# Four edits at the seams of a one-core kernel: start-up, down passes, first attention step, closing mix

## The chip, the core and the metric

The kernel runs on one core of one Trainium2 chip. The metric is the device time of one execution in microseconds (us); lower is better. The core has a matrix engine (PE, with PEld for its weight loads), two elementwise engines (DVE and ACT), a general engine (POOL), a queue engine (SP) and 16 DMA engines. SP, ACT and POOL can each issue DMAs, and each issues in the order of its own program.

## The reference, cut to what matters

```
x: [2048, 1024]   A_mem0: [8, 1024]   32 heads of 128   SEG = 32 -> 64 segments
g = sigmoid((x * gate_w).sum(-1))                    # one gate value per row
a: for each segment s, in order:
     h = concat(mem, x[32 s : 32 s + 32])            # 8 memory rows + 32 new rows
     q, k, v = h Wq, h Wk, h Wv                      # 1024 -> 32 heads x 128
     o = softmax(mask(q k^T / sqrt(128))) v ;  o = o Wo
     mem = o[0:8] ;  a rows of this segment = o[8:40]
b = (gelu(x Wg) * (x Wu)) Wd                         # 1024 -> 3584 -> 1024
out = g * a + (1 - g) * b
```

All tensors are bf16. Segment s + 1 needs the memory rows that segment s wrote, so attention is a chain of 64 steps.

## The kernel before, in words

A small planner class (`_Prog`) records every operation with the memory regions that it reads and writes. Each engine executes its operations in the order in which the code recorded them, and the class puts a semaphore wait on an operation wherever it depends on another engine or on a DMA. A DMA with a `lane` name also waits for the DMA before it in the same lane. So the order of the Python code is the order of each engine and of each queue, and a wait at the head of a queue holds up all that stands behind it there.

The work goes through four stages.

*Start-up.* Four tiles of x (128 rows each) are loaded on SP (`load_x`, L539). `do_x` turns each tile on PE (L550) into a PSUM bank. ACT (L557) and DVE (L558, L559) copy the turned tile out, ACT issues the stores of it to the scratch tensors `xq_scr` and `xr_scr`, POOL multiplies the tile with the gate weights (L566), and DVE sums the product (L568). `gate(0)` (L629 to L636) turns four sums into gate values and stores them from POOL, among others as single 4-byte values (`gt_scr`). Then the rows of the initial memory and the first segment are put together in `hT0` (`load_h`, L572, and the copy L663).

*Feed-forward stage.* Four blocks of 512 rows (`fb` 0 to 3). In each, 28 steps j run gate and up products on PE (L680) and a gelu on ACT and DVE (L688 to L696); the tile `xT` holds the block's input. Then two down passes (`ps` 0 and 1) of seven chunks each multiply the result with `w_down` (L732). A chunk is 16 matmuls of 128x512 and uses one 1 MB tile `wd`; there are three such tiles, and the load of the tile for chunk n + 3 (`load_wd`, L612, on SP) is issued when chunk n has been used. During the j steps of a block the four tiles of x of the next block are turned (`do_x`, at j = 3, 9, 15, 21), `gate` runs at j = 25, and in blocks 1 and 2 copies of attention weights between DRAM tensors are issued on SP (`spread`, L392). The load of `xT` for the next block (`load_xT`, L594, on SP, 1 MB) is issued after the last j. Results of the down passes are scaled and stored to `b_scr` (`mix`, L621 and L623).

*Attention steps.* The weights of k, q, v and o do not fit, so 50 slots of 4 KB per partition hold pieces of them; a slot whose piece has been used is loaded with the next one from SP (`spent`, L430). `walk` is the fixed order of the projections (L916, L932, L949) and `plan(s)` hangs the rest of step s at places in that order. The last 8 of each 32 new rows are projected four segments at a time in *fills* (L986): the result is copied out by ACT into a stage tile (`fill_evac`), and `fill_put` turns it on PE, copies it back on DVE and stores it from POOL to `qk_scr` (L1011, lane `fq`). In step 0 seven fills are done at once, with the stage tiles `kS`, `qS` and `oS`, which lie over `kT`, `qT` and `oT`. The step's scores (L839, L842) need part of `kT` that POOL copies (L1015) from `qkr`, which POOL loads back from `qk_scr` (L581). Each step stores its results to `a_scr` (L1129, on POOL).

*Closing stage.* `early` and the code after the walk load, for each of 16 row tiles T, 96 rows of `a_scr` (four DMAs of 96x256, L780) and 96 rows of `b_scr` (one DMA of 96x1024, L782), all on SP, into 6 pairs of buffers (`asb`, `bsb`). DVE mixes them with the gate (`blend`, L789) and ACT stores the rows (L792). The 8 remaining rows of each segment go through the output projection at the end (L1157, 256 matmuls) and are mixed at L1167.

In the profile the names of scratch tensors are shown without numbers, so `wall<-o_scr` is a weight piece of o read from its scratch copy, not the tensor `o_scr` of the steps.

Of the kernel before, what the change touches and what calls it, by code (L numbers as in the profile page):

```python
# [191 lines left out]
class _V:  # L192
# [11 lines left out]
    r = _T.r  # L204
# [6 lines left out]
def bass_gated_mix__memory_aug_recurrent_mem_tr__geglu_ffn__prompt_kernel(  # L211
# [34 lines left out]
    with ExitStack() as es:  # L246
# [16 lines left out]
        a_scr = nc.dram_tensor("a_scr", [NSEG, 4, SEG, 256], BF16)  # L263
# [254 lines left out]
        assert cur[0] == edge(50) and len(hosts) == 50  # L518
        tp = [al(f"tp{t}", [128, FB], FP32, at=qkr.off + 4 * FB * t) for t in range(2)]
# [21 lines left out]
        def do_x(T):  # L541
# [112 lines left out]
        load_w(1)  # L654
        for T in range(TB):
            do_x(T)
            load_x(T + NPX)
        gate(0)
# [3 lines left out]
        load_h(0, "pool")  # L662
        op("dve", lambda e: e.tensor_copy(hT0[:, :, NR:32], memT[:, :].rearrange("p (k c) -> p k c", k=KC)),  # L663
           rd=[memT.r()], wr=[hT0.r()])
        load_w(2)
        load_w(3)
        load_w(4)
        for n in range(3):
            load_wd()
        copies = [(m, u, i) for m in "ovkq" for u in (1, 0) for i in PAIRS[m]]  # L670
        todo = []
        for fb in range(NFB):
            HB, DN = ((0, 1, 2, 3), (4, 5, 6, 7)) if fb % 2 == 0 else ((4, 5, 6, 7), (0, 1, 2, 3))
            for j in range(NJ):
# [39 lines left out]
            if fb + 1 < NFB:  # L714
                load_xT(fb + 1)
            else:
                for n in (11, *range(20, 29)):
                    begin(n)
            for ps in range(NPS):
                bank = DN if ps == 0 else HB  # L720
                tbs = [x for x in (2 * ps, 2 * ps + 1) if x < TB]
                for c in range(NWD):
                    end = fb == NFB - 1
                    w = wdF if end else wd[((fb * NPS + ps) * NWD + c) % 3]
                    for jj in range(WD):
                        j = c * WD + jj
                        x = j if end else jj

                        def f(e, w=w, x=x, j=j, bank=bank, tbs=tbs):
                            for k, tb in enumerate(tbs):  # L730
                                for hf in range(2):
                                    ins = e.matmul(PB[bank[2 * k + hf]][:, :], lhsT=GT[:, j, tb * 128:(tb + 1) * 128],  # L732
                                                   rhs=w[:, x, hf * 512:(hf + 1) * 512], start=(j == 0), stop=(j == NJ - 1))
                            return ins
                        op("pe", f, rd=[GT.r(j * FB, (j + 1) * FB), w.r(x * D, (x + 1) * D)], wr=[BK(b) for b in bank[0:2 * len(tbs)]])
                        if j > 0 and todo:
                            mix(*todo.pop(0))
                    if not end:
                        load_wd()
                    elif ps == NPS - 1:  # L740
                        for n in (29 + 2 * c, 30 + 2 * c, 43 + c):
                            begin(n)
# [6 lines left out]
        oR = [al(f"oR{b}", [128, RB, 32], at=slots[home["q", 0, 0]].off + b * SB * 512) for b in range(NBK)]  # L749
# [7 lines left out]
        NA = 6  # L757
# [6 lines left out]
        assert cur[0] <= slots[home["v", 1, 5]].off  # L764
# [12 lines left out]
        def load_a(T):  # L777
            t, w = asb[T % NA], bsb[T % NA]
            for n in range(4):
                op("sp", lambda e, n=n: e.dma_start(t[0:NM, 256 * n:256 * n + 256], a_scr[4 * T:4 * T + 4, n, 0:NR, :]),  # L780
                   rd=[("D", "a", s) for s in range(4 * T, 4 * T + 4)], wr=[t.r(256 * n, 256 * n + 256)], lane=f"al{T % NA}{n}")
# [248 lines left out]
        def fill0(m, r, b, st, G=0, h=hR):  # L1030
            run(fill(m, r, b, h))
            fill_evac(m, r, G, b, st)
            fill_put(m, r, G, st)

        def plan(s):
# [44 lines left out]
            on(*(("q", 1, 1) if s else ("o", 0, 0)), lambda: evac(bank_of["k", 1], stage[ub if s else "k"], "act"))  # L1080
# [13 lines left out]
            else:  # L1094
# [4 lines left out]
                on("o", 0, 6, lambda: scores(ub, False))  # L1099
# [12 lines left out]
            if last:  # L1112
                for n, f in enumerate(early):
                    on(*((("v", 1, 4), ("o", 1, 0), ("o", 1, 1)) + (("o", 1, 2),) * 3)[n], f)
# [14 lines left out]
            on("k", 0, 4, lambda: op("pool", lambda e: e.dma_start(a_scr[s].rearrange("g r c -> (g r) c"), a_bf[:, :]), rd=[a_bf.r()],  # L1129
# [10 lines left out]
        op("pool", lambda e: e.dma_start(a_scr[NSEG - 1].rearrange("g r c -> (g r) c"), a_bf[:, :]), rd=[a_bf.r()],  # L1140
# [68 lines left out]
```

## Time and profile before

| what | value |
|---|---|
| time, median of 3 runs | 2300.27 us (2295.94 to 2300.56) |
| the profiled execution, its own time | 2304.75 us |
| its span, first to last instruction | 2302.9 us |
| PE busy | 2051.2 us, 89% of the span |
| DVE, ACT, POOL busy | 1042.1, 539.0, 434.2 us |
| start-up, until gate and up products run without a stall | 0 to 40 us |
| feed-forward stage | 40 to 649 us |
| attention step 0 | 650 to 709 us |
| steps 1 to 63 | 709 to 2178 us |
| closing stage | 2178 to 2303 us |

Busy time is the time in which an engine works on an instruction; it says nothing on what a stage waits for. Four views do: the chain that ended last, the sums of waits of an engine in a window, the timeline of a window, and the table of windows with the share of the 16 DMA engines in use.

### The profile page before, as it was taken

The page shows a single profiled execution, that of the slowest core. Times are in us where ns is not written, and L with a number is a line of the kernel's source. Part 1 is how long each engine was busy: PE and PEld are TensorE (multiplying, and loading weights), DVE is VectorE, ACT ScalarE, POOL GpSimd, SP SyncE. Part 2 cuts the span into 40 slices and gives each one's busy share as a digit, 9 for nine tenths or more (in the row PEclk, how much of TensorE's full clock was granted, in tenths as well). Part 3 has the DMA queues.
Part 4 walks back from the last instruction along what each step waited for, and adds up shares of the span by engine and source line. Part 5 has one row for each costly group of instructions (what it writes and reads, how often), then busy time and mean ns, then how long its engine had stood idle before and what let it go on. Part 6 is the DMA issues. An engine that isn't in the chain of part 4 may idle for free.

```text
span 2302.9 us, 69850 instructions
## 1 busy us (share of the span) xinstructions
PE 2051.2 (89%) x31365; PEld 975.8 (42%) x31365; DVE 1042.1 (45%) x2689; ACT 539.0 (23%) x1110; POOL 434.2 (19%) x839
## 2 busy tenths in 40 slices
PE   5999989999968999899999999999999989998880
PEld 2444434444424444444444444444444444444450
DVE  3624606516314445454545454555454544544412
ACT  2312303203112222222222222222222222222100
POOL 3000100000012222222222222222223222221100
PEclk8999999999989999999999999999999999998895
DMA  9255385293577899899999898999999989998932
GB/s 302 107 169 193 107 248 166 59 320 118 188 282 281 329 345 350 330 349 346 346 342 350 330 350 330 358 347 361 351 351 335 349 327 345 342 348 321 345 121 99
DMA packets 187871, 652.74 MB, mean 283 GB/s; under 512 B 22156, under 2 KB 78092, under 8 KB 146740
## 3 DMA queue, kind: packets, MB, share of 16 engines
q1 hardware_dynamic: 161060, 608.10, 72.6%
q0 software_dynamic: 14528, 26.32, 3.5%
q10 hardware_dynamic: 11984, 13.85, 1.7%
q8 instruction: 246, 4.03, 0.7%
q14 instruction: 53, 0.43, 0.1%
HBM read 613.64 MB, written 49.23 MB: 288 GB/s over the span
## 4 chain that ended last, share of the span: by engine, by line
PE 62%; DMA 21%; DVE 6%; SPq 5%; ACT 3%; issue 2%; POOL 1%; ACTq 0%; DVEq 0%; POOLq 0%
PE pb L916 24%; PE pb L680 13%; DMA wall<-o_scr 10%; PE pb L732 7%; PE pb L932 5%; PE pb L814 3%; SPq L780 3%; PE pb L949 3%; DMA o_scr<-oRc 3%; PE pb L986 2%; DMA wd<-in_B_w_down_dram 2%; DMA sl<-v_scr 1%; DVE oT L800 1%; PE pb L874 1%; DMA qk_scr<-1S 1%
## 5 line engine op out<-in xcount | busy, mean ns | idle before, releaser
L916 PE MATMUL pb<-sl,hT 128*32 128x512 bf16 x12288 | 763.9, 384 | 15.1 <-DVE hT L973 8.8
L916 PEld LDWEIGHTS pb<-sl,hT 128*32 128x32 bf16 x12288 | 308.5, 97 | 326.7 <-issue 27.7
L680 PE MATMUL pb<-xT,wg 128*128 128x512 bf16 x896 | 215.2, 384 | 21.8 <-DVE GT L696 15.6
L986 PE MATMUL pb<-sl,hR 128*32 128x512 bf16 x3072 | 212.9, 385 | 3.2 <-DVE osb L621 1.5
L680 PE MATMUL pb<-xT,wu 128*128 128x512 bf16 x896 | 212.3, 380 | 0.0
L949 PE MATMUL pb<-wall,oT 128*32 128x256 bf16 x4056 | 152.8, 280 | 28.0 <-DMA wall<-o_scr 23.7
L899 POOL COPY oRc<-oT 128x128 bf16<-128x128 bf16 x128 | 96.5, 754 | 402.4 <-DVE oT L800 402.4
L960 DVE COPY part<-pb 64x256 f32<-64x256 f32 x128 | 54.0, 422 | 257.4 <-PE pb L949 256.7
L732 PE MATMUL pb<-wd,GT 128*128 128x512 bf16 x672 | 154.1, 393 | 15.4 <-DMA wd<-in_B_w_down_dram 15.4
L932 PE MATMUL pb<-wall,oT 128*32 128x512 bf16 x2048 | 147.2, 386 | 5.8
L688 ACT ACTIVATE s<-pb 128x512 f32<-128x512 f32 x112 | 66.7, 596 | 325.1 <-PE pb L680 291.8
L680 PEld LDWEIGHTS pb<-xT,wg 128*128 128x128 bf16 x896 | 86.9, 99 | 129.0 <-DVE GT L696 21.4
L949 PEld LDWEIGHTS pb<-wall,oT 128*32 128x32 bf16 x4056 | 98.0, 98 | 87.8 <-ACT oT L797 26.7
L689 DVE SCALAR_TENSOR_TENSOR tp<-s,pb 128x512 f32<-128x512 f32 x112 | 76.9, 686 | 128.2 <-ACT s L688 128.2
L680 PEld LDWEIGHTS pb<-xT,wu 128*128 128x128 bf16 x896 | 88.0, 98 | 106.8 <-issue 1.9
L800 DVE COPY kT<-pb 128x512 bf16<-128x512 bf16 x128 | 54.4, 425 | 166.0 <-PE pb L814 165.6
L850 ACT ACTIVATE E<-pb 128x320 bf16<-128x320 f32 x128 | 56.0, 437 | 308.0 <-DVE pb L849 308.0
L797 ACT ACTIVATE oS<-pb 128x512 bf16<-128x512 f32 x65 | 38.8, 597 | 376.4 <-PE pb L916 367.7
L1015 POOL COPY kT<-qkr 128x128 bf16<-128x128 bf16 x128 | 37.3, 291 | 434.6 <-DVE tAB L862 219.3
L862 DVE STREAM_TRANSPOSE tAB<-pAB 128x128 bf16<-128x128 bf16 x512 | 114.1, 280 | 4.4
L693 DVE SCALAR_TENSOR_TENSOR tp<-tp,pb 128x512 f32<-128x512 f32 x112 | 77.0, 687 | 78.1 <-ACT tp L692 77.3
L732 PEld LDWEIGHTS pb<-wd,GT 128*128 128x128 bf16 x672 | 67.1, 101 | 102.0 <-DMA wd<-in_B_w_down_dram 18.6
(106 smaller groups left out, 2201.1 us busy)
## 6 DMA issues: line engine op xcount, KB each, us to landing
sl<-v_scr SPq DMA_DIRECT2D x64, 1536.0 KB, 9.9
wall<-o_scr SPq DMA_DIRECT2D x63, 1536.0 KB, 9.3
wall<-o_scr SPq DMA_DIRECT2D x131, 512.0 KB, 5.1
sl<-k_scr SPq DMA_DIRECT2D x64, 1024.0 KB, 5.5
sl<-q_scr SPq DMA_DIRECT2D x64, 1024.0 KB, 8.2
sl<-v_scr SPq DMA_DIRECT2D x64, 1024.0 KB, 9.4
wd<-in_B_w_down_dram SPq DMA_DIRECT2D x42, 1024.0 KB, 6.3
wdF<-in_B_w_down_dram SPq DMA_DIRECT2D x7, 1024.0 KB, 8.6
```

What stands on the lines that cost most here:

```text
L680: ins = e.matmul(PB[bk][:, 0:FB], lhsT=w[:, kc, cc:cc + 128], rhs=xT[:, :, :, kc, :].rearrange("p t i c -> p (t i) c"), start=(kc == 0), s ...
L689: op("dve", lambda e, hg=hg, t=t: e.scalar_tensor_tensor(out=t[:, :], in0=s1[:, :], scalar=1.0, in1=hg, op0=ALU.add, op1=ALU.mult), rd=[BK ...
L693: op("dve", lambda e, hu=hu, t=t: e.scalar_tensor_tensor(out=t[:, :], in0=t[:, :], scalar=1.0, in1=hu, op0=ALU.add, op1=ALU.mult), rd=[BK( ...
L732: ins = e.matmul(PB[bank[2 * k + hf]][:, :], lhsT=GT[:, j, tb * 128:(tb + 1) * 128], rhs=w[:, x, hf * 512:(hf + 1) * 512], start=(j == 0), ...
L780: op("sp", lambda e, n=n: e.dma_start(t[0:NM, 256 * n:256 * n + 256], a_scr[4 * T:4 * T + 4, n, 0:NR, :]), rd=[("D", "a", s) for s in rang ...
L800: op("dve", lambda e: e.tensor_copy(o, i), rd=rd, wr=wr, after=after)
L862: return [op("dve", lambda e, c=c: e.transpose(tAB[:, c + 32 * k:c + 32 * k + 4 * w].rearrange("p (j x) -> p j x", j=4)[:, :, 0:32], pAB[: ...
L899: op("pool", lambda e: e.tensor_copy(oRc[:, :, 16 * u:16 * u + 16].rearrange("p c x -> p x c"), oT[:, :, :, 32:40].rearrange("p g j c -> p ...
L916: ins = e.matmul(PB[bk][32 * g:32 * g + 32, :], lhsT=h[:, i, :], rhs=w[:, g * 512:(g + 1) * 512], start=(n == 0), stop=(n == 7))
L932: ins = e.matmul(PB[XO][32 * g:32 * g + 32, :], lhsT=oT[:, j, x, 0:32], rhs=wall[:, na:nb + 1:nb - na, c:c + 256], start=(n == 0 and hp == 0),
L949: ins = e.matmul(PB[XO][32 * g:32 * g + 32, 256 * b:256 * b + 256], lhsT=oT[:, j, x, 0:32], rhs=w[:, c:c + 256], start=False, stop=(n % 4 ...
L986: ins = e.matmul(PB[b][32 * g:32 * g + 32, :], lhsT=h[:, k[2], :], rhs=w[:, g * 512:(g + 1) * 512], start=(n == 0), stop=(n == 7))
```

## The change

Start-up: the four tiles are only turned (`do_x`); product and sum for the gate are a function of their own (`dot_x`), called in block 0 at j = 0 to 3, with the next tile's load, and `gate(0)` at j = 4. The weights of chunk 2 are loaded ahead of the second four tiles of x; those of chunks 3 and 4 and the first three `wd` after j = 3. `hT0` is put together in block 3 at j = 1. In later places `do_x` stands at j = 6, 11, 16, 21.

Down passes: the load of `xT` is issued in the second pass after chunk 3 of that pass, ahead of the `wd` load there.

Step 0: the fills have four stage tiles of their own, `X0` to `X3`, in the last weight slot (49), whose first load moves into step 0. The evacuations and the stores (`fill_put`) are hung at other places: for instance the fill of the second k half now comes before the first scores, and scores and attention of both halves stand later in the walk.

Closing stage: `a_scr` holds whole token rows. A step's store writes 128 pieces of 256 values into 32 rows; the loads of a row tile are one DMA of 96x1024. There are 14 pairs of buffers. The tiles `oR` lie in other slots, and the first load of them stands earlier in the last step.

```diff
-        a_scr = nc.dram_tensor("a_scr", [NSEG, 4, SEG, 256], BF16)
+        a_scr = nc.dram_tensor("a_scr", [NSEG, SEG, D], BF16)
...
+        for n in range(4):
+            stage[f"X{n}"] = al(f"X{n}", [128, 512], at=edge(49) + 1024 * n)
...
+        def dot_x(T):
+            t = px[T % NPX]
             op("pool", lambda e: e.tensor_tensor(out=gp[:, :], in0=t[:, :], in1=gwb[:, :], op=ALU.mult),
                rd=[t.r(), gwb.r()], wr=[gp.r()])
             op("dve", lambda e: e.tensor_reduce(dl[:, T:T + 1], gp[:, :], AX.X, ALU.add), rd=[gp.r()], wr=[dl.r(T, T + 1)])
...
         load_w(1)
+        load_w(2)
         for T in range(TB):
             do_x(T)
-            load_x(T + NPX)
-        gate(0)
...
-        load_h(0, "pool")
-        op("dve", lambda e: e.tensor_copy(hT0[:, :, NR:32], memT[:, :].rearrange("p (k c) -> p k c", k=KC)),
-           rd=[memT.r()], wr=[hT0.r()])
-        load_w(2)
-        load_w(3)
-        load_w(4)
-        for n in range(3):
-            load_wd()
+        def begin_h():
+            load_h(0, "pool")
+            op("dve", lambda e: e.tensor_copy(hT0[:, :, NR:32], memT[:, :].rearrange("p (k c) -> p k c", k=KC)),
+               rd=[memT.r()], wr=[hT0.r()])
...
-                T = TB * (fb + 1) + (j - 3) // 6
-                if fb < NFB - 1 and j in (3, 9, 15, 21):
+                if fb == 0 and j < TB:
+                    dot_x(j)
+                    load_x(j + NPX)
+                if fb == 0 and j == TB - 1:
+                    load_w(3)
+                    load_w(4)
+                    for n in range(3):
+                        load_wd()
+                if fb == 0 and j == TB:
+                    gate(0)
+                if fb == NFB - 1 and j == 1:
+                    begin_h()
+                T = TB * (fb + 1) + (j - 6) // 5
+                if fb < NFB - 1 and j in (6, 11, 16, 21):
                     do_x(T)
+                    dot_x(T)
                     load_x(T + NPX)
...
-            if fb + 1 < NFB:
-                load_xT(fb + 1)
-            else:
+            if fb + 1 == NFB:
...
                     if not end:
+                        if ps == NPS - 1 and c == 3:
+                            load_xT(fb + 1)
                         load_wd()
...
-        NA = 6
+        NA = 14
...
-            for n in range(4):
-                op("sp", lambda e, n=n: e.dma_start(t[0:NM, 256 * n:256 * n + 256], a_scr[4 * T:4 * T + 4, n, 0:NR, :]),
-                   rd=[("D", "a", s) for s in range(4 * T, 4 * T + 4)], wr=[t.r(256 * n, 256 * n + 256)], lane=f"al{T % NA}{n}")
+            op("sp", lambda e: e.dma_start(t[0:NM, :], a_scr[4 * T:4 * T + 4, 0:NR, :]),
+               rd=[("D", "a", s) for s in range(4 * T, 4 * T + 4)], wr=[t.r()], lane=f"al{T % NA}")
...
-                on("k", 0, 0, lambda: fill0("k", 0, B0, "k"))
-                if NG > 1:
-                    on("k", 0, 0, lambda: fill0("k", 0, B1, "o", 1, hR1))
-                on("q", 0, 0, lambda: fill0("q", 0, B1, "q"))
-                on("v", 0, 0, lambda: fill0("v", 0, B2, "o"))
+                on("k", 0, 0, lambda: fill0("k", 0, B0, "X0"))
+                on("k", 0, 0, lambda: fill0("k", 0, B1, "X1", 1, hR1))
+                on("k", 0, 0, lambda: fill_put("k", 0, 0, "X0"))
+                on("k", 0, 2, lambda: fill_put("k", 0, 1, "X1", SS))
+                on("q", 0, 0, lambda: fill0("q", 0, B1, "X2"))
+                on("q", 0, 2, lambda: fill_put("q", 0, 0, "X2"))
+                on("v", 0, 0, lambda: fill0("v", 0, B2, "X3"))
...
-                on("k", 1, 1, lambda: scores(ua, False))
-                on("k", 1, 1, lambda: attend(ua))
-                on("k", 1, 1, lambda: fill0("k", 1, B0, "k"))
-                on("q", 1, 0, lambda: fill0("q", 1, B1, "q"))
-                on("q", 1, 4, lambda: fill0("v", 1, B2, "k"))
+                on(*('k', 1, 4), lambda: scores(ua, False))
+                on("k", 1, 1, lambda: fill0("k", 1, A1, "X0"))
+                on(*('q', 1, 2), lambda: attend(ua))
+                on("k", 1, 4, lambda: fill_put("k", 1, 0, "X0"))
+                on("q", 1, 0, lambda: fill0("q", 1, B1, "X1"))
+                on("q", 1, 2, lambda: fill_put("q", 1, 0, "X1"))
+                on("q", 1, 4, lambda: fill0("v", 1, B2, "X2"))
+                on("o", 0, 4, lambda: begin(49))
...
-                on("o", 0, 6, lambda: scores(ub, False))
+                on(*('v', 1, 0), lambda: scores(ub, False))
...
-            on("k", 0, 4, lambda: op("pool", lambda e: e.dma_start(a_scr[s].rearrange("g r c -> (g r) c"), a_bf[:, :]), rd=[a_bf.r()],
+            on("k", 0, 4, lambda: op("pool", lambda e: e.dma_start(a_scr[s].rearrange("r (g c) -> g r c", g=4), a_bf[:, :]), rd=[a_bf.r()],
```

More of the change, by code (lines that the diff above doesn't have):

```diff
@@ L747, in bass_gated_mix__memory_aug_recurrent_mem_tr__geglu_ffn__prompt_kernel @@
         assert not copies and not any(done)
-        oR = [al(f"oR{b}", [128, RB, 32], at=slots[home["q", 0, 0]].off + b * SB * 512) for b in range(NBK)]
+        oR = [al(f"oR{b}", [128, RB, 32], at=(slots[home["k", 1, 5]].off + b * SB * 512) if b < 3 else slots[home["q", 0, 0]].off) for b in range(NBK)]
+        assert home["q", 1, 6] == home["k", 1, 5] + 7
         def load_oR(b):
@@ L763, in bass_gated_mix__memory_aug_recurrent_mem_tr__geglu_ffn__prompt_kernel @@
         gR = al("gR", [128, NBK], FP32)
-        assert cur[0] <= slots[home["v", 1, 5]].off
+        assert cur[0] <= edge(19)
         def load_gates():
@@ L1073, in plan @@
             if s == 0:
[L1074 to L1078 removed]
+                on(*('k', 1, 4), lambda: scores(ua, False))
[6 more added lines that the diff above has]
+                on("o", 0, 4, lambda: begin(49))
                 on("q", 1, 4, lambda: (load_qk(0, 1), load_v(0, slice(1, 2)), load_r(1) if NG > 1 else None))
[L1080 removed]
+            on("q", 1, 1, lambda: evac(bank_of["k", 1], stage[ub if s else "k"], "act"))
             if s > 0:
@@ L1113, in plan @@
                 for n, f in enumerate(early):
-                    on(*((("v", 1, 4), ("o", 1, 0), ("o", 1, 1)) + (("o", 1, 2),) * 3)[n], f)
+                    on(*((("v", 1, 0), ("o", 1, 0), ("o", 1, 1)) + (("o", 1, 2),) * 3)[n], f)
                 return
@@ L1139, in bass_gated_mix__memory_aug_recurrent_mem_tr__geglu_ffn__prompt_kernel @@
         ended = fold(NSEG - 1, 1)
-        op("pool", lambda e: e.dma_start(a_scr[NSEG - 1].rearrange("g r c -> (g r) c"), a_bf[:, :]), rd=[a_bf.r()],
+        op("pool", lambda e: e.dma_start(a_scr[NSEG - 1].rearrange("r (g c) -> g r c", g=4), a_bf[:, :]), rd=[a_bf.r()],
            wr=[("D", "a", NSEG - 1)], lane="st")
```

4 lines of the change are left out of this document (2 added, 2 removed).

## The prediction

> **What bounds the kernel now.** I read the page's slices first, then waits, chain and timeline of each stage that the diff touches. Waits of all engines, 0 to 62 us:
>
> ```profile
> DVE hT L663 <- DMA hT<-xq_scr: 16.9, 1, 16.9
> ...
> PE pb L680 <- DVE GT L696: 14.6, 1, 14.6
> ...
> PE pb L680 <- DVE xT L558: 5.3, 1, 5.3
> ```
>
> (total, times, longest.) DVE stands at the copy L663 until `hT` lands, so the gelu behind it stands still and PE has no bank for j = 2. PE's waits, 0 to 660 us:
>
> ```profile
> PE pb L732 <- DMA wd<-in_B_w_down_dram: 15.4, 5, 5.1
> ```
>
> Feed-forward is bound by PE but for this. Timeline of step 0:
>
> ```profile
> 665.66 0.60 ACT L797 ACTIVATE oS<-pb 128x512 bf16<-128x512 f32 x1 [6.36 <-DMA qk_scr<-oS]
> ...
> 673.13 0.60 ACT L797 ACTIVATE qS<-pb 128x512 bf16<-128x512 f32 x1 [6.38 <-DMA qk_scr<-qS]
> 673.33 0.56 POOL L581 DMA_DIRECT2D qkr<-qk_scr  x1 [4.29 <-DMA qk_scr<-qS]
> ...
> 676.84 0.33 PE L839 MATMUL pb<-kT,qT 128*32 128x40 bf16 x16 [0.67 <-POOL kT L1015]
> ...
> 698.92 0.40 PE L814 MATMUL pb<-ident,kS 128*128 128x128 bf16 x4 [4.18 <-ACT kS L797]
> ```
>
> Two things wait here: stages that are still being stored, and the lane of stores that ends in `qkr`. Closing stage, windows (us, busy of PE, PEld, DVE, ACT, POOL, clock, DMA share, GB/s), then DVE's waits, then the chain's start and a stretch of it:
>
> ```profile
> 2220.00:2230.00 10.00, 10.00 (x48) 6.70 (x47) 3.06 (x3) 0.00 (x0) 0.00 (x0) 1.00 0.27 93
> 2250.00:2260.00 10.00, 0.00 (x0) 0.00 (x0) 3.22 (x3) 0.00 (x0) 0.00 (x0) 0.50 0.31 105
> ```
>
> ```profile
> DVE bsb L789 <- DMA bsb<-b_scr: 91.5, 16, 16.0
> ```
>
> ```profile
> 2256.12 1.58 SPq L780
> 2257.75 1.64 SPq L780
> 2259.43 1.92 SPq L780
> 2261.39 1.29 SPq L780
> ...
> 2266.89 0.61 SPq L780
> 2267.55 0.62 SPq L780
> ```
>
> PE ends at 2238.5; the last 64 us are loads. The chain blames SP, but an issue costs 0.61 us when unhindered: five per tile are 3.3 of the 6.40 us that a tile takes (`bsb` issues 2223.88 to 2287.87, ten tiles). The rest is SP waiting for room. The DMA share of 0.27 to 0.31 is 4.3 to 5 engines of 16, whichever window; the packet records have four packets in flight for most of it. These transfers have four segments outermost. So four DMA engines are the bound.
>
> **The change part by part.** Sums go against the profiled execution: 2304.75 us, its span of 2302.9 and 1.85 around it; it lies 4.5 above the median of 2300.27.
>
> *Start-up.* Product (2.12) and sum (1.22) per tile leave the path from the turned tiles to PE. What is left per tile is ACT's copy 0.60, DVE's 0.42 and 0.28, and ACT's two issues 0.36 and 0.45, some 1.7 us; from 7.7 (first tile out) the fourth `xT` copy ends near 12.8, not 16.6. The first two j take 9.0 us as before (16.6 to 25.6, slow clock), so j = 2 starts at 21.8, not 40.18, at full clock: 3.46 a step, where the restart at 40.18 took 9.0 for two. End of j = 3: 28.7, not 49.1: 20.4 gained. Added: the four sums on DVE in j = 0 to 3. DVE needs 3 x 0.69 + 1.22 = 3.3 of 3.46 us per j; a bank is wanted again 5.2 us after its gate product, the gelu chain takes 3.4, and following the order step by step I get stalls of 0.4, 0.5, 0.5 and about 1.0 at the first `do_x`. Net -18. Ends: -20.4 (slack takes all) and -14 (sum and product in series, 4 x 3.3, less the slack of 4 x 1.8). Weights: in the packet records SP's first 4.7 MB had arrived by 20 us; now chunk 1 (wanted from 21.8) is still inside that, chunk 2 (3.7 MB at 385 GB/s) comes by 30 (wanted at 39), x tile 4, now behind it on SP, by 31 (wanted at 38), chunk 3 is issued near 33 and wanted at 66, chunk 4 at 90: covered, also with 10 us lost to `gate(0)`'s stores, which now fall here; each us late would cost one. The moved `do_x` and `gate(0)` issue what they issued. `hT` is now loaded by POOL behind the third block's gate stores (446), 60 us before the copy: 0.18 us of DVE.
>
> *xT.* Now: after the last j, `xT` (1 MB) goes ahead of the fourth `wd` and lands after 11.7 to 12.7 us; PE stands 4.1, 5.1 and 4.5 us in the three first passes. Bytes hardly move there, though `xT` is alone; the DMA view of 130 to 150 us, in slices of 0.5 us:
>
> ```profile
> GB/s 3 1 1 1 1 1 0 0 0 0 111 106 45 0 25 16 8 12 25 16 4 4 29 41 119 205 393 401 410 406 418 401 393 389 393 393 381 377 385 381
> ```
>
> In the packet records the same happens to the chunk-2 weights from 26 to 34 us, and each time 6 to 14 us after POOL's gate stores (4-byte values) began at 20.5, 129.2, 284.5, 443.5; I blame those, and they stay. So the fourth `wd` gains only the 2.7 us that `xT` takes at 390 GB/s: -8. In the second pass `xT` stands ahead of the last `wd`, which in block 0 already landed with no slack (issue 178.94, 6.99 us, PE waited 0.2): 2.7 there, about 2.2 in the others: +7. `xT` itself has 10.4 us before its use. Net -1; ends -10 (no new stall) and +10 (third rival).
>
> *Step 0.* With own stages nothing waits for a store before a copy-out (6.4, 6.4, 3.7 us on ACT), but the lane stays: three stores of 5.5, 5.8 and 7.2 us, now starting 1.1 us later, as the first turn stands behind the second fill. First scores 677.9 (from 676.8). PE fills the wait with the k fill, then q; first attention ends near 682.7. Then the lane again: k store issued at 682.9 (DVE is in the softmax), q store at 687.5, `qkr` back near 695.5, second scores 696 instead of 702.7, attention 700.9 instead of 706.9: -6. Ends -10 (stores of 4.3, the median) and 0 (lane slower by as much). SP's wait for slot 49 (stores of `X1`, `X2`, until 695) stands ahead of the o group load and step 1's `qkr`; before they were issued at 702 to 703, so 0; if the stores come later than 702, us for us.
>
> *Closing stage.* Packet records: 512 bytes took 27 ns, 2048 took 84. Per tile an engine had 24 x (4 x 27 + 2 x 84) = 6.62 us, now 24 x 3 x 84 = 6.05; at the measured 6.40 that is 5.85, and 16 x 0.55 = -9. 48 SP issues fewer and eight more buffers: 0, since the four engines already worked without a gap from 2197; only the start (2188 to 2197) could close up. PE's 2.5 us wait for `oR` goes, 64 us off the path: 0. The chain from last landing to end (2296.5 to 2302.9) stays. Ends -6 and -14.
>
> The Trainium skill (DMA: Bandwidth & Descriptors, section "Why a DMA increments its semaphore by 16 and not by 1") says that a DMA runs on the largest number of engines up to 16 that divides the slowest dimension of both sides. For 96 rows against four segments that is four, before and after; the share of 0.27 to 0.31 agrees.
>
> *The step's store of `a_scr`.* Its outermost dimension also becomes four. If that confines it as it does the closing loads, four engines get 4 x 159 ns in place of 159 (4096-byte packets): 0.48 us per step, at most 63 x 0.48 = 30; at least 0. It is issued right after PE's wait for o weights has ended (1043.65 after 1041.3) and PE waits for those weights 21.6 us in all from 800 to 2160, so I take a tenth: +3. POOL's issue stays near 0.55, as `v_scr` stores show. By the same section of the Trainium skill the store would use four engines and lose up to those 30 us, a point against this change; no run here shows it.
>
> Sum: -18 - 1 - 6 - 9 + 3 = -31, so 2273.7 for such an execution and 2269 on the median.
>
> **The rivals.**
> 1. *The closing stage opens.* If SP's issues or a fixed cost per DMA were the bound, 48 fewer would leave PE's end, 2238.5, plus some 8 us: -56 in place of -9, 2222. For it: 56% of the chain from 2140 us on is SP. Against: the 0.61 us floor, the constant share. The Trainium skill (DMA: Bandwidth & Descriptors, section Rules for kernel authors) says that DMAs under 64 KB pay mostly overhead and should be merged; 48 KB ones become 192 KB ones, and by that rule it is this rival.
> 2. *Steps get slower* (the other side). Place: the 63 `a_scr` stores. (31 + 3 + 4.6 for 0.2%) / 63: from 0.6 us per step it decides. If 128 scattered rows hurt as the 576 tiny gate packets did (some 8 us, so 14 ns each), 1.8 us per step: 2380. Against: `v_scr` and `qk_scr` stores of 256-byte pieces land in 4.3 and 5.7 us, this one in 7.0.
> 3. *`xT` is slow by itself.* Then it takes 12 us in the second pass too, and the last `wd` behind it 14.7 against 6.9: +23 for three blocks, -13.7 in the first passes, +10 in place of -1: 2280. For it: the delay starts with `xT`. Against: the weights at 26 to 34 us.
> 4. *Start-up stalls elsewhere* (late weights, DVE): half the gain, 2278.
>
> **How the numbers follow.** Forecast 0.66 (its own range 2255 to 2284), rivals 0.08, 0.05, 0.12, 0.09. Leaving out most of rivals 1 and 2 and the forecast's edges gives 2242 to 2288. Within 0.2% (4.6 us) a measurement of this kernel can't be told from no change. Faster 0.93, same 0.02, slower 0.05.
>
> **What would show it.** PE's wait for GT at the start below 3 us and the first L680 near 13; no `hT` wait on DVE; first-pass `wd` waits of 1 to 2 us and new ones at the last chunk; from the first fill to the second scores 46 us (650.0 to 702.7 before); from SP's last `oRc` store (2177.7) to the end 116 us, not 125, the share still near 0.3; steps at the same 23.3 us (2177.7 less 708.8, over 63). A share above 0.5 in the closing stage or longer steps would prove me wrong.

## The result, and the profile after

The changed kernel takes 2270.42 us in the median of four runs (2264.33 to 2282.65), the kernel before 2300.41 beside it: a ratio of 0.9879, 95% interval 0.9835 to 0.9923. A second comparison with more runs (label `after_again` below) gave 0.9844, 0.9808 to 0.9880. So the change is worth 28 to 36 us by these two, and 18 to 44 by their intervals. 2269 was forecast.

The profiled execution of the changed kernel took 2264.33 us (span 2262.5). It is the fastest of its four, and that of the kernel before is 4 us over its median, so the two profiles are 40.4 us apart and a comparison of these two alone says too much. Where a stage is judged below, its time comes from all profiles with and without the edit.

PE's waits in the changed kernel, 0 to 660 us (total, times, longest):

```profile
PE pb L743 <- DMA wd<-in_B_w_down_dram: 11.4, 7, 2.2
PE pb L854 <- POOL kT L1030: 7.6, 1, 7.6
...
PE pb L680 <- DVE GT L696: 2.8, 2, 1.9
```

The wait of 14.6 us for GT is gone, and so is DVE's wait for `hT`. The five waits for `wd` of up to 5.1 us are seven of up to 2.2. In step 0 PE now stands 7.6 us for `kT` ahead of the first scores (L854), which begin 27.3 us behind the first fill (26.8 before, 27.9 forecast). The start still holds a wait that the prediction had not seen. Timeline of ACT at the start, changed kernel:

```profile
10.43 0.60 ACT L559 ACTIVATE xT<-pb 128x512 bf16<-128x512 bf16 x1 [1.63 <-DVE hR L561]
14.05 0.33 ACTq L563 DMA_DIRECT2D xq_scr<-xT  x1
14.41 0.44 ACTq L566 DMA_DIRECT2D xr_scr<-xr  x1
14.90 0.60 ACT L559 ACTIVATE xT<-pb 128x512 bf16<-128x512 bf16 x1 [3.87 <-DMA xq_scr<-xT]
```

The third copy is done at 11.0, but its store (L563) is issued at 14.05: it has a lane together with the store of the first tile and stands until that one has landed. The fourth copy stands behind it on ACT. Step 0, POOL and then PE of the changed kernel:

```profile
665.37 0.56 POOL L585 DMA_DIRECT2D qkr<-qk_scr  x1
670.52 0.55 POOL L589 DMA_DIRECT2D vB<-v_scr  x1 [4.59 <-DMA v_scr<-X]
671.07 0.56 POOL L580 DMA_DIRECT2D hR<-xr_scr  x1
```

```profile
672.07 0.33 PE L854 MATMUL pb<-kT,qT 128*32 128x40 bf16 x16 [5.98 <-POOL kT L1030]
...
676.83 1.47 PE L1001 MATMUL pb<-sl,hR 128*32 128x512 bf16 x12 [4.30 <-DMA hR<-xr_scr]
```

The second scores (L854) begin at 672.07, 45.6 us behind the first fill, as forecast (46; 52.7 before). Behind them PE meets a new wait: `hR` is loaded by POOL behind the load of v, which waits for v's stores, and PE stands 4.3 us for it. The closing stage, windows of the changed kernel (us, busy of PE, PEld, DVE, ACT, POOL, clock, DMA share, GB/s) and DVE's wait:

```profile
2190.00:2200.00 10.00, 9.95 (x47) 6.67 (x47) 3.22 (x3) 0.00 (x0) 0.00 (x0) 1.00 0.30 112
...
2220.00:2230.00 10.00, 0.00 (x0) 0.00 (x0) 2.99 (x3) 0.00 (x0) 0.00 (x0) 0.50 0.30 111
```

```profile
DVE bsb L804 <- DMA bsb<-b_scr: 84.7, 16, 15.5
```

The share is as low as before (0.27 to 0.31 there). A tile now takes 5.95 us, not 6.40, by the starts of DVE's mixes; PE is done at 2205 and 57 us of loads follow.

### The profile page after: what moved, and what is told of

It reads as the page before. It is cut to its first block, busy times and chain, and to the rows that moved or that the text cites. A ratio compares the mean times of both kernels' runs of the same rounds, so it can differ in the third digit from the quotient of the medians.

```text
span 2262.5 us, 69748 instructions
## 1 busy us (share of the span) xinstructions
PE 2035.5 (90%) x31339; PEld 973.6 (43%) x31365; DVE 1040.7 (46%) x2689; ACT 539.7 (24%) x1110; POOL 445.4 (20%) x839
## 4 chain that ended last, share of the span: by engine, by line
PE 59%; DMA 25%; DVE 5%; SPq 4%; ACT 3%; issue 2%; POOL 2%; ACTq 0%; DVEq 0%; POOLq 0%
PE pb L931 21%; PE pb L680 15%; DMA wall<-o_scr 9%; PE pb L743 7%; PE pb L947 4%; PE pb L829 3%; DMA sl<-v_scr 3%; PE pb L964 3%; DMA wd<-in_B_w_down_dram 3%; DMA qk_scr<-1S 2%; PE pb L1001 2%; DMA o_scr<-oRc 2%; SPq L795 2%; DMA qk_scr<-0S 1%; DMA v_scr<-kS 1%
## 5 line engine op out<-in xcount | busy, mean ns | idle before, releaser
L964 PE MATMUL pb<-wall,oT 128*32 128x256 bf16 x4056 | 149.7, 276 | 22.6 <-DMA wall<-o_scr 18.4
L743 PE MATMUL pb<-wd,GT 128*128 128x512 bf16 x657 | 148.8, 385 | 12.2 <-DMA wd<-in_B_w_down_dram 11.4
L688 ACT ACTIVATE s<-pb 128x512 f32<-128x512 f32 x112 | 66.8, 596 | 315.5 <-PE pb L680 278.9
L815 DVE CAST oT<-pb 128x160 bf16<-128x160 f32 x256 | 76.3, 319 | 77.4 <-PE pb L897 77.4
```

The costliest lines, as they stand in the source:

```text
L815: op("dve", lambda e: e.tensor_copy(o, i), rd=rd, wr=wr, after=after)
L964: ins = e.matmul(PB[XO][32 * g:32 * g + 32, 256 * b:256 * b + 256], lhsT=oT[:, j, x, 0:32], rhs=w[:, c:c + 256], start=False, stop=(n % 4 ...
```

## The experiments

All stage times that the experiments gave stand in one table. Each is read from PE's and SP's timeline: the first product with `w_down`; from there to the first fill; from there to the store of `oRc` of step 0; from there to that of step 63; and from there to the end of the span.

| profile | start-up and block 0's gate and up | rest of feed-forward | step 0 | steps 1 to 63 | closing |
|---|---|---|---|---|---|
| before | 133.8 | 516.2 | 58.8 | 1468.8 | 125.2 |
| only_start | 116.3 | 509.2 | 60.2 | 1465.6 | 127.2 |
| only_xT | 131.5 | 501.4 | 60.5 | 1472.1 | 125.1 |
| only_step0 | 131.6 | 509.6 | 57.8 | 1472.7 | 126.4 |
| only_close | 131.8 | 509.1 | 57.1 | 1465.1 | 118.5 |
| after | 117.7 | 508.8 | 57.4 | 1458.6 | 120.0 |
| after_again | 116.1 | 501.8 | 56.7 | 1458.1 | 119.2 |
| old_store | 116.0 | 503.8 | 57.4 | 1473.3 | 127.8 |
| xT_one_later | 116.2 | 498.1 | 56.2 | 1468.8 | 119.0 |
| small_three | 114.5 | 503.6 | 52.7 | 1465.5 | 119.5 |
| rmajor_before | 131.4 | 509.8 | 58.9 | 1478.1 | 87.6 |
| rmajor_after | 116.7 | 502.2 | 59.2 | 1468.5 | 67.1 |
| rmajor_6_pairs | 116.0 | 504.1 | 56.8 | 1454.9 | 66.8 |
| together | 113.8 | 495.7 | 51.7 | 1468.0 | 66.8 |

### The four parts alone

`only_start`: of the diff in "The change" it has the hunks of start-up, in the kernel before. Edit, cut short:

```diff
+        load_w(2)
         for T in range(TB):
             do_x(T)
-            load_x(T + NPX)
-        gate(0)
...
+                if fb == 0 and j < TB:
+                    dot_x(j)
+                    load_x(j + NPX)
```

> The kernel before with the start-up edit alone (the gate's products and sums behind the gate and up products of j = 0 to 3, later chunks loaded after j = 3, the first hT in the last block, do_x at j = 6, 11, 16, 21). Theory: the parts are independent, and this one is worth what the stage showed, 16 us: down pass of block 0 at 117 to 118 us in place of 133.8, everything after it shifted by the same, 2284 us (2280 to 2288). Rival, the gain needs the other parts (for instance because the xT load at the end of block 0 collides with the later gate stores): the first down pass gives back 4 us or more, 2288 and above.

Measured: 2278.86 us, ratio 0.9911 (0.9883 to 0.9939), 20 us faster by the ratio, a little more than the 16 expected; the time lies 1 us below the expected range. The down passes of block 0 begin at 116.3 (117 to 118 expected) and give nothing back: from their first product to the first gate product of block 1 they take 53.7 us, 55.6 before. So the start-up edit pays by itself, and the rival falls.

`only_xT`:

```diff
-            if fb + 1 < NFB:
-                load_xT(fb + 1)
...
+                        if ps == NPS - 1 and c == 3:
+                            load_xT(fb + 1)
                         load_wd()
```

> The kernel before with the xT load moved into the second down pass, behind chunk 3, and nothing else. The feed-forward stage from the first down pass to the first fill took 516.2 us before and 508.8 after. Theory: all of these 7.4 us are this edit's, the waits for wd in the first passes fall from 4.1, 5.1 and 4.5 us to 1 to 2 us and new ones of 1 to 2 us come at the last chunk; 2293 us (2290 to 2297). Rival (xT is slow by itself): the wait goes to the last chunk in full, 2300 or more.

Measured: 2284.40 us, ratio 0.9952 (0.9931 to 0.9972), 11 us faster and below the expected range (2290 to 2297); the stage takes 501.4 us. PE's waits for `wd` in its profile, 0 to 640 us:

```profile
PE pb L730 <- DMA wd<-in_B_w_down_dram: 8.2, 10, 2.6
```

In the first passes of blocks 0 to 2 PE waits 0.45, 0.29 and 0.51 us (3 to 5 each in all profiles without the edit); at the last chunk it waits 2.57, 0.44 and 1.68 instead. So the edit pays, and the rival (`xT` slow by itself) falls. The 516.2 us of the first profile of before were high: without this edit four other profiles have 509.1 to 509.8.

`only_step0`: the stage tiles `X0` to `X3` and the order of step 0.

```diff
-                on("k", 0, 0, lambda: fill0("k", 0, B0, "k"))
+                on("k", 0, 0, lambda: fill0("k", 0, B0, "X0"))
+                on("k", 0, 0, lambda: fill0("k", 0, B1, "X1", 1, hR1))
+                on("k", 0, 0, lambda: fill_put("k", 0, 0, "X0"))
...
-                on("k", 1, 1, lambda: scores(ua, False))
+                on(*('k', 1, 4), lambda: scores(ua, False))
```

> The kernel before with the four stage tiles X0 to X3 and the new order in step 0 alone. From the first fill to the oRc store of step 0: 58.84 us before, 57.42 after. Theory from the trace of after: second scores come 7 us sooner, then PE waits 4 us for hR, which POOL loads only behind a load that waits for v_scr stores, and the attention gains 1 to 2 us in all: 2299 us (2296 to 2301), inside what can't be told from no change. Rival (the prediction's own figure): 6 us, 2294.

Measured: 2293.07 us, ratio 0.9989 (0.9970 to 1.0008): no difference that can be told from nothing, but the interval also holds the 6 us of the rival. The stage decides: step 0 takes 57.8 us, 1.3 below the mean of the profiles without the edit (59.1), so the theory fits and the 6 us don't.

`only_close`: `a_scr` by rows, one load per tile, 14 pairs, `oR` moved.

```diff
-        a_scr = nc.dram_tensor("a_scr", [NSEG, 4, SEG, 256], BF16)
+        a_scr = nc.dram_tensor("a_scr", [NSEG, SEG, D], BF16)
...
-        NA = 6
+        NA = 14
```

> The kernel before with a_scr kept by token rows, one 192 KB load per tile, 14 pairs of buffers and the moved oR alone. Theory A: the closing stage gains 5 us (120 from the last oRc store to the end, 125 before; a tile every 5.95 us in place of 6.40) and the steps stay at 23.3 us each; the 10 us that steps 1 to 63 lost between the two profiles come and go with the execution: 2295 us (2292 to 2299). Theory B: those 10 us belong to the store of a_scr or to the code moved with it; steps at 23.15 us, 2285 (2281 to 2289).

Measured: 2284.41 us, ratio 0.9953 (0.9930 to 0.9975), 11 us faster; closing 118.5. The steps take 1465.1 us, between the 1468 of theory A (63 at 23.3) and the 1458 of theory B (63 at 23.15), so this run left the question of the steps open.

The four ratios multiply to 0.981, some 45 us, with an uncertainty of several us for each.

### The changed kernel again

No edit.

> The changed kernel itself, timed against the kernel before with more runs. Alone the four parts gave ratios of 0.9911, 0.9952, 0.9989 and 0.9953, 45 us in all, the whole 0.9879 (28 us) in a first comparison of four runs each. Theory A: the parts add, and the first comparison had too few runs: a ratio of 0.979 to 0.983. Theory B: the xT edit and the start-up edit share a gain (feed-forward from the first down pass to the first fill 501.4 us with the xT edit alone, 508.8 with all): 0.985 to 0.989.

Measured: 2260.42 us, ratio 0.9844 (0.9808 to 0.9880), between the two theories. Its feed-forward stage takes 501.8 us with the same code that took 508.8 in the first profile, so the shared gain of theory B, which rested on that number, isn't there. Within the uncertainties the parts add.

### What bounds the closing stage

`rmajor_after`: the rows of a tile are taken row by row and, within a row, segment by segment, in both loads, the gate and the output's store. The bytes and the number of DMAs stay.

```diff
-            op("sp", lambda e: e.dma_start(t[0:NM, :], a_scr[4 * T:4 * T + 4, 0:NR, :]),
+            op("sp", lambda e: e.dma_start(t[0:NM, :], a_scr[4 * T:4 * T + 4, 0:NR, :].rearrange("s r c -> r s c")),
```

> The changed kernel with the rows of a tile in the closing stage in another order, the 24 rows outermost and the 4 segments inside them, in the loads of a_scr and b_scr, in the gate gM and in the store of the output; the same bytes in the same number of DMAs. Theory (the prediction's: four outermost segments put each of these DMAs on four engines): the 24 rows spread over more, 12 engines if it is the largest number up to 16 that divides 24 and 96; a tile takes about 2 us in place of 5.95, the loads end before PE does, and the closing stage is PE's 55 us behind its start plus 7: some 70 us from the last oRc store to the end in place of 120, 2270 - 50 = 2220 us. Rival (a cost per DMA, or SP): the same DMAs cost the same, 120 us, 2270.

Measured: 2215.77 us, ratio 0.9649 (0.9610 to 0.9688), 45 us below the changed kernel. Windows of its closing stage, then the last two results that DVE mixes:

```profile
2170.00:2180.00 10.00, 10.00 (x48) 6.69 (x47) 6.14 (x6) 0.00 (x0) 0.00 (x0) 1.00 0.83 293
2180.00:2190.00 10.00, 10.00 (x48) 6.63 (x47) 8.03 (x8) 0.00 (x0) 0.00 (x0) 1.00 0.83 313
```

```profile
2202.92 0.75 DVE L1186 SCALAR_TENSOR_TENSOR orb<-pb,gR,brb 128x512 bf16<-128x512 f32 x1 [2.39 <-PE pb L1176]
...
2209.82 0.75 DVE L1186 SCALAR_TENSOR_TENSOR orb<-pb,gR,brb 128x512 bf16<-128x512 f32 x1 [4.97 <-PE pb L1176]
```

The share goes from 0.30 to 0.83, the rate from 112 to 313 GB/s, and at the end DVE waits for PE, not for loads. In the packet records, without those of 4 bytes, exactly four packets are in flight for 74% of the time between 2175 and 2240 us of the changed kernel; here 12 for 45% and 13 for 30% of it between 2170 and 2198. The Trainium skill (DMA: Bandwidth & Descriptors, section "Why a DMA increments its semaphore by 16 and not by 1") gives the number of engines as the largest up to 16 that divides the slowest dimension on both sides; for 24 and 96 that is 12, for 4 and 96 it is 4. These are the commonest counts in the records; the 13 is one more than the rule gives, and where that one comes from stays open.

`rmajor_before`: the same order of rows in the kernel before.

```diff
-                op("sp", lambda e, n=n: e.dma_start(t[0:NM, 256 * n:256 * n + 256], a_scr[4 * T:4 * T + 4, n, 0:NR, :]),
+                op("sp", lambda e, n=n: e.dma_start(t[0:NM, 256 * n:256 * n + 256], a_scr[4 * T:4 * T + 4, n, 0:NR, :].rearrange("s r c -> r s c")),
```

> The kernel before with the same other order of rows; it keeps four loads of 96x256 and one of 96x1024 per tile and six pairs of buffers. Theory (four engines were the bound): the engines need 6.4 x 4/12 = 2.1 us per tile, SP's five issues at 0.61 us now bound it at 3.3, so 16 tiles end about when PE does: 72 to 80 us in the closing stage in place of 125, 2296 - 50 = 2246 us. So the merged load and the eight buffers would be worth nothing much by themselves. Rival 1 of the prediction (SP's issues or a fixed cost per DMA): no change, 2296 us.

Measured: 2259.85 us, ratio 0.9830 (0.9783 to 0.9877), 37 us faster; the closing stage takes 87.6 us, more than the 72 to 80 expected. SP in its timeline:

```profile
2225.70 3.16 SPq L780 DMA_DIRECT2D asb<-a_scr  x4
2228.91 0.76 SPq L782 DMA_DIRECT2D bsb<-b_scr  x1
2229.71 3.15 SPq L780 DMA_DIRECT2D asb<-a_scr  x4
2232.90 0.76 SPq L782 DMA_DIRECT2D bsb<-b_scr  x1
```

Here SP issues without a gap, five in 4.0 us, and a tile takes these 4.0 us: an issue costs 0.76 us, 0.80 with the gap behind it, and not 0.61. The price goes with the order of rows and not with issuing back to back: in `rmajor_6_pairs` an issue behind a pause of 1.5 us takes 0.76 too (at 2166.07), and in the kernel before two in a row take 0.61 and 0.62 (the lines of the prediction). Four engines were the bound of the kernel before, and SP stood behind them. Rival 1 of the prediction is wrong for the change as made and right one step further on.

`rmajor_6_pairs`: `rmajor_after` with six pairs of buffers.

```diff
-        NA = 14
+        NA = 6
```

> The changed kernel with the 24 rows outermost in the closing stage and six pairs of buffers in place of 14. With the merged load SP issues two DMAs per tile and not five. Theory: SP's issues alone made the older kernel with the same order of rows stand at 4.0 us per tile (five at 0.80 us back to back, 87.6 us from the last oRc store to the end); two at 0.8 leave the stage to PE with six pairs too: 67 to 70 us. Rival: the buffers were what opened it, 78 us or more.

Measured: 2204.78 us, ratio 0.9602 (0.9579 to 0.9625); closing 66.8 us. The merged load is what the order of rows needs beside it; the eight more pairs of buffers bring nothing. The Trainium skill (DMA: Bandwidth & Descriptors, section Rules for kernel authors) asks to merge DMAs of less than 64 KB; here the merging belongs to a gain of 7 us while four engines were the bound (126.4 to 119.2), and of 21 us once they weren't (87.6 to 66.8).

### Three small waits

`small_three`:

```diff
-               rd=[xo[1](0, 4)], wr=[("D", "xq", T)], lane=f"xw{x2}")
+               rd=[xo[1](0, 4)], wr=[("D", "xq", T)], lane=f"xw{T % 4}")
...
-                if fb < NFB - 1 and j == 25:
-                    gate(fb + 1)
+                if fb in (1, 2) and j == 8:
+                    gate(fb)
+                if fb == 2 and j == 25:
+                    gate(3)
...
-                on("q", 1, 4, lambda: (load_qk(0, 1), load_v(0, slice(1, 2)), load_r(1) if NG > 1 else None))
+                on("q", 1, 4, lambda: (load_qk(0, 1), load_r(1) if NG > 1 else None, load_v(0, slice(1, 2))))
```

> The changed kernel with three small edits in three stages. (1) The stores of the turned tiles to xq_scr at the start have four lanes in place of two: theory, ACT's 3.9 us wait goes and the first gate product is at 13 us in place of 16; rival, the fourth copy waits for something else, 15 or later. (2) The gates of blocks 1 and 2 are worked out and stored at j = 8 of their own block and no longer at j = 25 of the block before; that of block 3 stays at j = 25 of block 2. Theory (the 4-byte gate stores starve the loads for 8 to 14 us): the first passes of blocks 0 and 1 lose their waits for wd, block 2's stays at 1 to 3 us; rival (the load of wd or xT is slow by itself there), no difference between the blocks. (3) In step 0 POOL loads hR before it loads v: theory, PE's 4.3 us wait for hR shrinks below 1 and step 0 takes 54 us in place of 57.4; rival, the wait turns into one for v of the same length, 57. In all 2 to 8 us below the changed kernel.

Measured: 2255.35 us, ratio 0.9814 (0.9773 to 0.9855), 5 us below `after_again`, with intervals that overlap; so each edit is read in its own stage.

(1) The first gate product is at 13.08 us, as forecast by the theory and, for the changed kernel, by the prediction. ACT's copies in its timeline no longer wait for a store:

```profile
10.03 0.60 ACT L559 ACTIVATE xT<-pb 128x512 bf16<-128x512 bf16 x1 [1.41 <-PE pb L552]
11.12 0.33 ACTq L563 DMA_DIRECT2D xq_scr<-xT  x1
11.48 0.44 ACTq L566 DMA_DIRECT2D xr_scr<-xr  x1
11.97 0.60 ACT L559 ACTIVATE xT<-pb 128x512 bf16<-128x512 bf16 x1 [1.35 <-DVE xr L561]
```

(2) The DMA view has the rate in 40 slices of 0.5 us. The changed kernel from 115 to 135 us (first down pass from 117.7), then `small_three` in the same place from 112 to 132 (first down pass from 114.5, no gate stores ahead of it), then `small_three` from 415 to 435 us (from 417.2, with gate stores):

```profile
GB/s 1 1 1 0 0 0 0 0 0 0 0 0 0 0 16 8 61 12 25 20 70 94 49 131 291 369 401 422 397 418 393 397 381 389 389 385 389 393 242 139
```

```profile
GB/s 0 0 0 0 0 0 0 0 0 0 0 0 0 0 86 61 115 352 401 406 410 402 98 209 369 401 401 406 193 61 164 397 418 414 410 287 180 233 369 397
```

```profile
GB/s 1 1 1 131 0 0 0 0 0 0 0 0 0 41 119 152 221 98 86 254 238 365 397 234 311 315 397 401 414 274 356 356 365 377 283 213 123 303 332 377
```

With the stores ahead, the load needs 5.5 us from its first bytes to 350 GB/s (block 2, the third line: 4 us); without them 1.5 us. The first `wd` load of the three windows lands 9.1, 5.4 and 7.0 us after its issue. That is the slow start that the prediction put down to the gate's 4-byte stores, and it is gone where they are gone. The stores themselves land only 7 to 10 us after their issue, so they are still under way when the load starts. All this costs PE little by now: in the first passes there is no wait for `wd` in blocks 0 and 1 and one of 0.6 us in block 2, where 1 to 3 were expected to stay, and the stage (503.6 us) is no shorter than in `after_again` (501.8).

(3) POOL and PE of `small_three` in step 0:

```profile
657.62 0.56 POOL L585 DMA_DIRECT2D qkr<-qk_scr  x1
658.18 0.56 POOL L580 DMA_DIRECT2D hR<-xr_scr  x1
662.75 0.55 POOL L589 DMA_DIRECT2D vB<-v_scr  x1 [4.01 <-DMA v_scr<-X]
```

```profile
663.73 0.32 PE L856 MATMUL pb<-kT,qT 128*32 128x40 bf16 x16 [5.40 <-POOL kT L1032]
663.86 0.33 PE L859 MATMUL pb<-kT,qkr 128*32 128x160 bf16 x4
663.96 1.51 PE L1003 MATMUL pb<-sl,hR 128*32 128x512 bf16 x12
```

The wait for `hR` is gone, and step 0 takes 52.7 us, some 5 below the mean of the profiles of the new step 0 without this edit (57.4).

### xT one chunk later

```diff
-                        if ps == NPS - 1 and c == 3:
+                        if ps == NPS - 1 and c == 4:
                             load_xT(fb + 1)
```

> The changed kernel with the xT load issued after chunk 4 of the second down pass and no longer after chunk 3, so behind the last wd of that pass and ahead of the first of the next. Theory: the waits at the last chunk (2.2, 1.0 and 2.2 us; 2.8, 0.6 and 1.9 in a second profile) go, xT still lands in the two chunks that are left (7.1 us for 1 MB behind 1 MB), and the feed-forward stage from the first down pass to the first fill takes 497 to 499 us in place of 502 to 509. Rival: xT now lands too late and PE waits for it at the first gate product of the next block, no gain or a loss of up to 3 us per block.

Measured: 2263.78 us, ratio 0.9837 (0.9807 to 0.9866); the stage takes 498.1 us. PE's waits for `wd`, 0 to 640 us:

```profile
PE pb L743 <- DMA wd<-in_B_w_down_dram: 4.2, 4, 1.4
```

None is left at a last chunk. For `xT` PE's weight loads wait once, 0.3 us at the first gate product of block 3, so the rival is out. The stage behaves as in the theory. The total does not show it: the steps of this execution (1468.8 us) are longer than those of `after_again`, and the 3 us lie inside the interval.

### The store of a step

`old_store`: the changed kernel with the old rows of `a_scr` (the old declaration, four loads per tile, six pairs).

```diff
-            on("k", 0, 4, lambda: op("pool", lambda e: e.dma_start(a_scr[s].rearrange("r (g c) -> g r c", g=4), a_bf[:, :]), rd=[a_bf.r()],
+            on("k", 0, 4, lambda: op("pool", lambda e: e.dma_start(a_scr[s].rearrange("g r c -> (g r) c"), a_bf[:, :]), rd=[a_bf.r()],
```

> The changed kernel with a_scr kept as before (a step's store writes one run of 64 KB; four loads of 96x256 per tile in the closing stage, six pairs of buffers), all else as changed. It asks what the rows of a_scr are worth in the steps. Steps 1 to 63 took 1465.6 to 1478.1 us in the five profiles with the old store (mean 1471.4) and 1458.1 to 1468.5 in the five with the new one (mean 1463.1). Theory B: the new store makes the steps some 8 us shorter, and with 6 to 7 us of the closing stage this kernel is 14 to 15 us slower than the changed one, with steps of 1466 us or more in its profile. Theory A: the steps differ by chance, 6 to 7 us slower, steps anywhere from 1458 to 1478.

Measured: 2278.25 us, ratio 0.9908 (0.9886 to 0.9930), some 15 us slower than the changed kernel at 0.9844, 7 at the 0.9879 of the first comparison; steps 1473.3 us. All six profiles with the old store have 1465.6 to 1478.1 us (mean 1471.8), all eight with the new one 1454.9 to 1468.8 (mean 1463.4). The ranges overlap, and the spread inside the two groups leaves the difference of 8 us uncertain by some 6. So theory B: with the new store the steps are shorter, by some 8 us; that it is chance is unlikely, but the size is rough. Why isn't settled. The store itself gets slower (7.0 to 7.4 us to landing in the six, 8.7 to 9.0 in the eight), as the issues of `only_step0` (old store) and of `only_close` (new one) show (KB each, median us to landing):

```profile
a_scr<-a_bf POOLq DMA_DIRECT2D x64, 64.0 KB, 7.2
```

```profile
a_scr<-a_bf POOLq DMA_DIRECT2D x64, 64.0 KB, 9.0
```

Over the steps PE waits less for o weights (25.8 us in the mean of the old, 22.6 of the new) and for ACT's copies of `0S` and `1S` ahead of their turns (17.1 and 12.5), together 7.8 us less, while other waits grow by some 2 us and PE's busy time in the steps falls from 1347.9 to 1345.4 us in the mean. The share of the DMA engines is 0.92 to 0.93 in the steps, and a store that spreads over more time may disturb the loads less. That is argued, not shown.

### All of it together

The edits of `rmajor_6_pairs`, `small_three` and `xT_one_later` in one kernel.

> The changed kernel with all of the small edits that were tried: 24 rows outermost with six pairs, four store lanes at the start, the gates of blocks 1 and 2 at j = 8 of their own block, hR ahead of v in step 0, xT after chunk 4. Theory: the stages are independent, so the sum of what each showed by itself: the kernel with 24 rows outermost and six pairs had a ratio of 0.9602 (2205 us), less 2 us at the start, 5 in the feed-forward stage and 4 in step 0, 2194 us (2188 to 2200), a ratio of 0.955; start-up to 114.5, feed-forward to 498, step 0 53, closing 67. Rival: what one stage gains, the next gives back as a wait for DMA (the steps are bound by transfers, share 0.92), 2200 or more.

Measured: 2196.54 us (2186.64 to 2197.81), ratio 0.9545 (0.9515 to 0.9576): faster than both kernels, 101 us below the one before. Its stages are as expected (113.8, 495.7, 51.7, 66.8). Only the steps, 1468.0 us in this profile, are at the upper end of their group.

## Why the prediction was right, step by step

The time was forecast as 2269 us and is 2270.4 in the first comparison and, at 0.9844 of 2300.3, 2264 by the second. The sum was right, but its terms were off in both directions, three of them by 4 us and more: gains that were put 9 us too high in all at the start, in step 0 and in the closing stage stand against 17 to 18 us put too low at `xT` and the store. That the total came out so close is luck; the mechanisms of the four parts are mostly right, that of the store isn't. Against the means of the profiles with and without each edit:

| step | forecast | measured |
|---|---|---|
| start-up | -18 | -15.6 (132.0 to 116.4) |
| xT | -1 | -7.1 (510.8 to 503.7) |
| step 0 | -6 | -1.7 (59.1 to 57.4) |
| closing | -9 | -7.1 (126.4 to 119.2) |
| store of a_scr, in the steps | +3 | -8.4 (1471.8 to 1463.4) |
| sum | -31 | -39.9 |

The measured sum is a few us above the timed 28 to 36; the means of few profiles, each step with a spread of several us, don't carry that difference.

*Start-up.* The mechanism was right: PE's waits for GT fell to 2.8 us, none of them at the start (both in blocks 1 and 2), so the feared stalls of 2.4 us stayed away, and no `hT` wait is left. Mis-sized was the piece ahead of PE: the first product was forecast near 13 and stands at 15 to 16, since the third store of a turned tile waits in its lane for the first. Two issues of 0.36 and 0.45 us had been counted on ACT, but not the wait of the first of them: 3.9 us. `small_three` (13.08) shows that this was all. Rival 4, half the gain, is out.

*xT.* The direction of both halves was right and both sizes were off. The fourth `wd` was to gain 2.7 us per block; its wait of 3 to 5 us is all but gone in `only_xT` (0.45 at most) and 0 to 2.3 in the two profiles of the changed kernel. The last chunk was to lose 7 us in three blocks; the waits there are 4.7 in `only_xT`, 5.4 in `after`. Rival 3 is out by the ratio of `only_xT`. The cause named for the slow start of the loads, the gate's stores, is confirmed by `small_three`.

*Step 0.* The second scores came at 45.6 us against 46 forecast; the step that failed is the next one, "attention 700.9 instead of 706.9". The attention stands at 55.6 us behind the first fill, not at the 50.9 forecast (56.9 before). The prediction followed `qkr` to the end of its lane and not what PE's order puts between scores and attention: a fill of the next group, whose `hR` POOL loads behind a load that waits. When a stall goes, the next thing that is late decides, and to see it one would have had to follow POOL's order here.

*Closing.* Four engines are the bound, as forecast, and the experiment on the order of rows shows it. The tile was mis-sized by 0.1 us (5.95 against 5.85), and there are 15 intervals between the 16 mixes of DVE, not 16: from the first mix to the last it takes 93.1 us, 99.4 before. That the eight buffers and the saved issues are worth nothing there fits this change, whose tile gained 0.45 us where the packets alone were to give 0.55; `rmajor_before` shows that the issues would have counted as soon as more engines took part, and with 0.80 us each, not 0.61.

*The store.* Forecast at +3 between 0 and 30; it is a gain of 8, outside the range that was given to it. A gain had been excluded without a reason, where a bound below zero belonged. That POOL's issue would stay near 0.55 us was wrong too: it takes 0.73 now, off the path. Rival 2, the steps that get slower, is out; its price per scattered row was taken from 576 tiny packets of the gate, where the records show some 80 of 4 bytes and 64 of 32 in one set.

## What to carry to other kernels

Look at a low, constant DMA share together with the number of packets in flight. Here they showed how many DMA engines took part (share 0.30 with four packets in flight, 0.83 with 12 and more), and the order of two dimensions in the access pattern, at no cost in bytes, tripled that number and was worth more than the whole change. When a wait is removed, follow the order of every queue that feeds the next consumer, the lanes of stores included: at the start and in step 0 the gain fell short because a copy or a load stood in a queue behind something that it didn't need. A bound on one cost hides the next one close behind it; four engines hid SP's issues, and only both edits together leave PE as the bound.

## What the runs showed that had not been expected

- The scattered store of `a_scr` (128 pieces of 512 bytes) lands 1.8 us later than the contiguous one (9.0 against 7.2) and yet the steps are some 8 us shorter with it, by 14 profiles. The cause is open.
- One set of gate stores leaves some 80 packets of 4 bytes and 64 of 32 in 3 us in the records, lands only 7 to 10 us after its issue, and holds up a load that follows: 4 to 5.5 us from its first bytes to 350 GB/s with them, 1.5 us without.
- An SP issue of these 96-row loads costs 0.61 us in the kernel before, and 0.76 in `rmajor_before` and `rmajor_6_pairs`, where the rows stand in the other order, with a pause ahead of it or without.
